# A convolution stem's backward pass: the second input gradient chains its shared products in PSUM, and the order of all operations becomes a written list

## The chip, the cores and the metric

The kernel runs on one core of a Trainium2 chip. The metric is the device time of one execution in microseconds (us), as a median over runs. Five engines work side by side and meet through semaphores: TensorE (PE: matmuls into PSUM, with its weight loads, PEld), VectorE (DVE), ScalarE (ACT), GpSimd (POOL) and SyncE (SP). In this kernel SP issues nearly all DMAs and DMA transposes, POOL the stores of transposed gradient pieces (`dld`). Each engine works through its own instructions in the order in which they were written.

## The reference

A strided one-dimensional convolution with group norm (one group a channel) and GELU, and its vector-Jacobian product:

```python
# x (2, 16000, 256), w (31, 256, 256), grad_out (2, 7985, 256), all bf16
h = sum(einsum('blc,cd->bld', x[:, i:i + 2*L:2, :], w[i]) for i in range(31))   # L = 7985
mu, var = mean and variance of h over l, for each b and d
out = gelu((h - mu) / sqrt(var + 1e-5) * gn_gamma + gn_beta)                   # tanh form
_out, _vjp = jax.vjp(_f, x, w, gn_gamma, gn_beta)
return (out, *_vjp(grad_out))          # out, d/dx, d/dw, d/dgamma, d/dbeta
```

## The kernel before, in words

The program has five stages, which are also the names in its planner: F0 and F1 (forward convolution of batch elements 0 and 1), G0 (the elementwise GELU work and input gradient of element 0), G1 (input gradient of element 1, from the end of element 0's on) and W (the weight gradient). Elementwise work of one stage runs under the matmuls of another.

**The input gradient** (`input_grad`) runs over 2 batch elements, 4 chunks `c`, 2 halves `pr` and 3 branches in the order B, A, C: 24 branches for each element. The convolution is split by fast-convolution identities: a branch has three leaves B, A, C, where leaf B is shared and the results are "B plus A" and "B plus C"; the outputs of branch B are in turn added to those of the branches A and C. `g_sums` makes the differences of input planes on DVE (`first`, `second`, `third`, all through L1282). `slots4` gives each branch two PSUM slots of two banks each, `px` and `pt`; four slots rotate, so a branch uses again what the branch two before it used, with the two slots exchanged.

For a branch of element 0 the steps are: `g_three_b`, four matmuls of 512 columns into the first bank of `px`, and an ACT copy of that bank to the second one (L1356); `g_three_ac`, eight matmuls of difference terms on both banks; `g_seed`, here one ACT copy of `px` into `pt`; then, inside the next branch's steps, `last(A)` and `last(C)`, which add the leaves A and C and evacuate them with `g_evac`: branch B's results into an fp32 tile `GRB` (ACT), the others by a DVE addition with `GRB` into the output tile `HO` (L1428). After branch C the tile goes out in one DMA of 1 MB.

For element 1 (`GOC` holds all its halves) the leaves A and C are split once more: `g_outer` makes a shared product of four matmuls for each of them (with weight sums `W2DO` and `W2DC`, made by `w2_outer`), into the two banks of `pt`, and eight matmuls of difference terms replace sixteen. `g_seed` then joins everything on DVE in fp32: an operation of 2048 elements that adds `GRB` to both products, spread over both banks (in branch B an ACT copy, L1392, instead), and one of 2048 that adds `px` and writes `pt` and `px` (both L1396). As `GRB` is already in the seed, `g_evac` is a plain ACT copy to `HO` (`keep`, L836). A branch has 36 matmuls.

**The order.** The code above only lists operations with their dependencies (`plan.add`). `Plan.order` gave each a due time, from a cost model and two long tables of leads per kind (`lead`, `fine`), and `listing` laid out the five engines by due time in a small model of the chip. `emit` then writes them in that order, so the list fixes the order on each engine. PE runs through helpers with one line per stage: L741 forward, L1329 input gradient, L1564 weight gradient. L683 and L687 are weight differences and sums, L699 the forward's plane sums, L1101 to L1129 the GELU unit, L1211 to L1231 `e_comp`, the elementwise gradient of a half-tile: two loads (`hd`, `dyd`), scalings (on ACT for the last two chunks of element 1, L1218 and L1220), an addition, four copies into the plane tile (L1231). For element 1 all half-tiles share one pair of load buffers, so a load waits until the last of these four copies has read it. L547 is any load or store, L552 a DMA transpose.

## Time and profile before

| what | us |
|---|---|
| runs: lowest, median, highest of 3 | 1164.47, 1166.46, 1167.01 |
| profiled execution: its span, first to last instruction | 1161.2 |
| what lies around the span, against the median of the runs | 5.3 |
| PE busy, DVE busy, ACT busy, POOL busy | 1128.5, 982.8, 554.0, 131.7 |
| matmuls of the input gradients (L1329), first and last start | 417.8, 847.3 |
| `g_seed` on DVE (L1396), first and last start | 655.3, 838.8 |

The profiled execution's own device time is not listed apart from its span; the three runs lie 3.3 to 5.8 us above it. The page gives each engine's busy time, the span in 40 slices, the DMA queues, the chain of work that ended last, and the costliest groups of instructions; the trace behind it answers further views: groups by line and shape (busy us, mean ns of one, idle time before them and what ended it), waits (who waited for whom), the chain of waits in order of time, the timeline (with the idle time before an instruction in brackets) and busy times in windows. Matmuls are pipelined and their ends are modelled.

### The profile page before, as it was taken

To read this page: it belongs to the slowest core of one execution; us is meant where nothing else is said; L and a number is where in the kernel's file an instruction comes from. 1 tells how busy PE (TensorE), PEld (TensorE's weight loads), DVE (VectorE), ACT (ScalarE), POOL (GpSimd) and SP (SyncE) were. 2 spreads that over 40 slices of the span, in tenths; PEclk is the share of its full clock that TensorE was granted. 3 is DMA by queue.
4 is the path that set the end of the run, shared out by engine and by line. 5 is a ranking of instruction groups with operands and counts; after the bars stand their busy time and mean duration, and the time that the engine had idled before them with its cause. 6 is when DMAs were issued, how large, how long until landed. Compare 5 with 4: busy or idle time off the path is not lost.

```text
span 1161.2 us, 18913 instructions
## 1 busy us (share of the span) xinstructions
PE 1128.5 (97%) x7700; PEld 753.2 (65%) x7700; DVE 982.8 (85%) x892; ACT 554.0 (48%) x833; POOL 131.7 (11%) x221
## 2 busy tenths in 40 slices
PE   5999999999999999999899999999999999999998
PEld 3888899877777864444344444444488766656685
DVE  7996787699989988998786868768799998699986
ACT  1254454688786588788563545653422212211200
POOL 0000000000000011333232132241200000000000
PEclk9999999999999999999999999999999999999999
DMA  9476738869796699999996886686999726899673
GB/s 217 63 184 127 179 109 164 208 140 200 182 248 141 221 366 255 261 263 231 256 228 192 179 191 163 159 200 175 212 353 289 256 82 221 287 323 320 219 222 104
DMA packets 345807, 243.57 MB, mean 210 GB/s; under 512 B 233377, under 2 KB 316967, under 8 KB 341543
## 3 DMA queue, kind: packets, MB, share of 16 engines
q1 hardware_dynamic: 338615, 223.47, 73.5%
q0 software_dynamic: 7104, 18.89, 6.1%
q8 instruction: 60, 0.98, 0.4%
q14 instruction: 28, 0.23, 0.1%
HBM read 106.24 MB, written 80.25 MB: 161 GB/s over the span
## 4 chain that ended last, share of the span: by engine, by line
PE 80%; DVE 6%; DMA 6%; ACT 3%; SPq 3%; issue 2%; DVEq 0%; ACTq 0%
PE ps L741 33%; PE ps L1329 24%; PE ps L1564 22%; DMA arena<-dld 2%; SPq L547 2%; DMA out_dram<-arena 1%; DMA arena<-hd 1%; SPq L552 1%; DVE arena L1428 1%; ACT arena L836 1%; DMA arena<-dyd 1%; DVE arena L1116 1%; DVE arena L1282 1%; DVE arena L687 1%; DMA arena<-in_x_dram 1%
## 5 line engine op out<-in xcount | busy, mean ns | idle before, releaser
L1329 PE MATMUL ps<-arena 128*128 128x512 bf16 (+1 forms) x1920 | 414.0, 377 | 9.8 <-DVE arena L1428 3.2
L741 PE MATMUL ps<-arena 128*128 128x256 bf16 (+4 forms) x3460 | 406.8, 281 | 14.7 <-DMA arena<-in_x_dram 6.0
L741 PEld LDWEIGHTS <-arena 128*128 128x128 bf16 x3460 | 338.1, 99 | 83.2 <-DVE arena L683 6.4
L1329 PEld LDWEIGHTS <-arena 128*128 128x128 bf16 x1920 | 188.3, 98 | 233.6 <-issue 16.9
L1564 PE MATMUL ps<-arena 128*128 128x256 bf16 (+1 forms) x2320 | 309.2, 296 | 4.1 <-DMA arena<-dld 2.3
L1564 PEld LDWEIGHTS <-arena 128*128 128x128 bf16 x2320 | 226.8, 98 | 86.8 <-DMA arena<-dld 2.1
L836 ACT ACTIVATE arena<-ps 128x1024 f32<-128x1024 f32 (+1 forms) x111 | 113.1, 1022 | 248.9 <-PE ps L1564 86.1
L699 DVE TENSOR_TENSOR arena<-arena 128x2080 bf16<-128x2080 bf16 (+8 forms) x126 | 157.1, 1266 | 27.1 <-PE ps L741 26.4
L547 POOL DMA_DIRECT2D dld<-arena x144 | 104.6, 728 | 295.1 <-DMA arena<-arena 247.8
L1116 DVE TENSOR_TENSOR arena<-arena 128x2048 bf16<-128x2048 bf16 (+1 forms) x80 | 95.6, 1196 | 11.9 <-ACT arena L1110 5.8
L1282 DVE TENSOR_TENSOR arena<-arena 128x1032 bf16<-128x1032 bf16 (+1 forms) x120 | 84.5, 727 | 12.7 <-PE ps L1329 6.6
L1532 DVE TENSOR_TENSOR arena<-arena 128x4096 bf16<-128x4096 bf16 x38 | 86.1, 2285 | 7.9 <-DMA arena<-in_x_dram 5.5
L1396 DVE TENSOR_TENSOR ps<-ps,arena 128x2048 f32<-128x2048 f32 x24 | 55.1, 2298 | 22.3 <-PE ps L1329 21.4
L856 ACT ACTIVATE arena<-ps 128x512 bf16<-128x512 f32 (+1 forms) x64 | 37.0, 580 | 57.9 <-PE ps L741 53.7
L556 POOL MEMSET arena<- 128x128 bf16 (+11 forms) x40 | 8.6, 246 | 403.6 <-ACT ps L777 149.3
L1666 ACT COPY ps<-ps 128x256 f32<-128x256 f32 x54 | 19.3, 358 | 73.2 <-PE ps L1564 72.1
L1396 DVE TENSOR_TENSOR arena<-ps,arena 128x2048 f32<-128x2048 f32 x16 | 36.6, 2290 | 18.7 <-ACT arena L836 15.3
L1356 ACT COPY ps<-ps 128x512 f32<-128x512 f32 x48 | 27.5, 577 | 44.5 <-PE ps L1329 38.6
L1106 DVE SCALAR_TENSOR_TENSOR arena<-arena 128x2048 bf16<-128x2048 bf16 (+1 forms) x16 | 35.8, 2238 | 12.1 <-ACT arena L1103 12.1
L1428 DVE TENSOR_TENSOR arena<-ps,arena 128x1024 bf16<-128x1024 f32 x32 | 38.8, 1219 | 7.7 <-DMA out_dram<-arena 4.6
L1735 DVE TENSOR_TENSOR arena<-arena 128x4608 bf16<-128x4608 bf16 x16 | 40.5, 2552 | 5.7 <-PE ps L1564 5.6
L777 ACT ACTIVATE ps<-ps 128x256 f32<-128x256 f32 x75 | 27.8, 371 | 36.4 <-PE ps L741 35.1
(83 smaller groups left out, 780.4 us busy)
## 6 DMA issues: line engine op xcount, KB each, us to landing
arena<-in_x_dram SPq DMA_DIRECT2D x40, 1024.0 KB
dld<-arena POOLq DMA_DIRECT2D x144, 128.0 KB, 3.8
arena<-hd SPq DMA_DIRECT2D x32, 512.0 KB
out_dram<-arena SPq DMA_DIRECT2D x14, 1024.0 KB
arena<-dld SPq DMA_DIRECT2D x18, 640.0 KB
arena<-dld SPq DMA_DIRECT2D x18, 576.0 KB
vl<-arena SPq DMA_DIRECT2D x36, 256.0 KB
arena<-vl SPq DMA_DIRECT2D x9, 1024.0 KB
```

What stands on the lines that cost most here:

```text
L547: lambda: e.dma_start(out=out, in_=in_), dma=np_ * ns / 16e3 * 1.03, ns=ns, tp=SH[pk], slack=slack)
L699: lambda: nc.vector.tensor_tensor(out=o, in0=a, in1=b, op=ALU.add))
L741: yield nc.tensor.matmul(ps[:, dh, cs], lhsT=wt, rhs=mv, start=s0, stop=False, skip_group_check=True)
L836: lambda: nc.scalar.activation(out=out, in_=ps, func=ACT.Copy, scale=scale))
L1116: add("DVE", dve(nf), [o], [a, b_], lambda: V.tensor_tensor(out=o, in0=a, in1=b_, op=op))
L1282: lambda: nc.vector.tensor_tensor(out=o, in0=a, in1=b, op=ALU.subtract))
L1329: yield nc.tensor.matmul(ps[:, e, 0:wide], lhsT=lt, rhs=mv, start=s0, stop=False, skip_group_check=True)
L1396: lambda: nc.vector.tensor_tensor(out=o, in0=a, in1=b, op=ALU.add))
L1428: lambda: nc.vector.tensor_tensor(out=ho[:, :, k, :], in0=ps[:], in1=g, op=ALU.add))
L1532: add("DVE", dve(4096), [o], [a, b], lambda: nc.vector.tensor_tensor(out=o, in0=a, in1=b, op=ALU.add))
L1564: yield nc.tensor.matmul(ps[:, s, c0:c1], lhsT=lt, rhs=mv, start=s0, stop=False, skip_group_check=True)
L1735: add("DVE", dve(4608), [o], [u, v], lambda: nc.vector.tensor_tensor(out=o, in0=u, in1=v, op=ALU.subtract))
```

## The change

For element 1, a branch now runs like this. The C product (with `W2DC`) goes into the first bank of `pt`; ACT copies it into the first bank of `px` (`g_copy`). `g_three_b` adds its four matmuls onto that copy (`fresh` is false) and ACT copies the sum to the second bank of `px`. The A product, with weights that are now negated sums, is added onto the C product in `pt`, so that `pt` holds C minus A; ACT copies that to SBUF (`g_delta`, two fp32 tiles `GSD` in turn). After the difference terms, one DVE operation of 1024 elements writes `pt` = `px` minus `GSD`. The branch sums leave the seed: branch B is evacuated into a bf16 tile `GSB`, the others into `HO` by ACT as before, and after leaf C one DVE addition in bf16 of 2048 elements adds `GSB` to the branch's two slices of `HO`. There are two `HO` tiles for element 1; element 0 keeps to one. All of `second` and the joined `third_two` (both leaves' differences in one DVE instruction of 2064 elements) are listed ahead of the first product. Matmuls per branch stay 36. `w2_outer(A)` uses a negating scalar_tensor_tensor instead of an addition. Switches that were empty (`GLAST`) are gone.

The planner's tables and model are gone too. `SEQUENCE` is a written list of all 3252 operations, by their number in the order in which the code adds them (there were 3224), and `order` returns it. It differs from the order before in every stage, forward and weight gradient included.

```diff
+SEQUENCE = """
+6 12 5 7 13 9 4 11 8 17 1 22 16 2 15 14 32 35 31 34 38 40 33 37 36 41 25 42 39 43 44 26 47 46 50 45 49 52 53 27 51 54 55 56 30 48 62 23 67 66 24 61
+29 68 87 28 86 85 18 89 84 20 88 72 21 19 75 59 64 65 58 83 60 73 92 63 57 93 69 91 94 95 179 70 90 177 71 79 236 100 74 97 101 78 102 96 103 10 111
...
+2043 2008 2018 2007 2055 2044 2079 2045 2019 2046 2013 2118 2012 2119 2015 2011 2017 2127 2009 2016 2080 2048 1470 2021 2123 2010 2026 2121 2004 2022
+2120 2049 2023 2050 2028 2024 2025 2060 2051 2207 2061 2052 2020 2030 2053 2054 2027 2031 2206 2131 2032 1477 2029 2036 2126 2033 2062 2122 2076 2211
...
     def order(self):
...
+        seq = [int(i) for i in SEQUENCE.split()]
+        assert sorted(seq) == list(range(len(self.ops)))
+        seen = set()
+        for i in seq:
+            assert self.ops[i]["preds"] <= seen
+            seen.add(i)
+        return seq
...
+    HO = [sb(119232, 2, 4, 512), sb(GREG + 16704, 2, 4, 512)]
+    GSB = sb(115136, 2, 2, 512)
+    GSD = [sb(o, 512, dt=FP32) for o in (111040, 113088)]
...
-    def g_three_b(ps, br, lf, pl, o):
+    def g_three_b(ps, br, lf, pl, o, fresh=True):
...
-        g_mm(ps, jobs, [ps[:, 0]], [wd, pl[1]])
-        add("ACT", act(512), [ps[:, 1]], [ps[:, 0]],
-            lambda: nc.scalar.copy(out=ps[:, 1], in_=ps[:, 0]))
+        g_mm(ps, jobs, [ps[:, 0]], [wd, pl[1]] + ([] if fresh else [ps[:, 0]]))
+        g_copy(ps[:, 1], ps[:, 0])
+
+    def g_copy(o, i):
+        add("ACT", act(512), [o], [i], lambda: nc.scalar.copy(out=o, in_=i))
...
+        jobs = [(0, 512, pl[1][:, dh, o + q2:o + q2 + P], wd[:, dh, 1 - q2, :], lf == C_ and q2 + dh == 0)
                 for q2 in range(2) for dh in range(2)]
-        g_mm(pt, jobs, [pt[:, k]], [wd, pl[1]])
+        g_mm(pt, jobs, [pt[:, 0]], [wd, pl[1]] + ([] if lf == C_ else [pt[:, 0]]))
...
+    def g_delta(pt):
+        gsc[0] += 1
+        g_copy(GSD[gsc[0] % 2], pt[:, 0])
+
+    def g_seed(px, pt, both):
+        if not both:
+            keep(flat2(pt), flat2(px))
+            return
+        t = GSD[gsc[0] % 2]
+        i = bass.AP(tensor=t.tensor, offset=t.offset, ap=[list(t.ap[0]), [0, 2], [1, 512]])
+        add("DVE", dve(1024, 1), [pt[:]], [px[:], t],
+            lambda: nc.vector.tensor_tensor(out=pt[:], in0=px[:], in1=i, op=ALU.subtract))
...
         if both:
...
             keep(ho[:, :, k, :], ps[:])
+            if lf == C_:
+                v, g = ho[:, :, r2:r2 + 3:2, :], GSB.rearrange("p l e f -> p e l f")
+                add("DVE", dve(2048), [v], [v, GSB], lambda: nc.vector.tensor_tensor(out=v, in0=v, in1=g, op=ALU.add))
...
+                        if both:
+                            if pr == 0:
+                                second(br, C_)
+                                second(br, A)
+                                third_two(br)
+                            g_outer(pt, br, planes(br, C_), o, C_)
+                            g_copy(px[:, 0], pt[:, 0])
+                        g_three_b(px, br, B_, planes(br, B_), o, not both)
...
+                        if both:
+                            g_outer(pt, br, planes(br, A), o, A)
+                            g_delta(pt)
+                        g_three_ac(px, br, B_, GU[br], o)
```

In the list's first two lines, 61 to 85 are the first weight differences and plane sums of the forward pass (83 is the weight difference that PE's matmul group 92 reads, 63 the one that 90 and 91 read). In the two lines further down stands the first branch of element 1: 2021 is its C product and 2022 the copy, 2023 the B product and 2024 the copy, 2028 the A product and 2029 the copy, 2030 and 2031 the difference terms, 2036 the subtraction; 2025, 2026, 2032 and 2033 are the leaves of the branch before (eight matmuls each, as that branch is of element 0) and 2034 the evacuation of its leaf C; 2068, 2075 and 2076 are leaf groups of this branch (four matmuls each); 2051 to 2054 are the four copies of an `e_comp`, 2206 and 2207 the loads of the half-tile after it, 2211 one of its scalings; 2064, in the line after these, is the next branch's C product.

470 lines of the change are left out of this document (40 added, 430 removed), and 98 rows, old and new, of the table SEQUENCE.

## The prediction

> **What bounds the kernel now.** I read the page's head first, then the waits of TensorE (PE) over the whole span, the busy times in windows of 50 us over the second input gradient, the groups by line and shape, and last the timeline and the chain of waits at the places where PE stood still.
>
> ```profile
> span 1161.2 us, 18913 instructions
> PE 1128.5 (97%) x7700; PEld 753.2 (65%) x7700; DVE 982.8 (85%) x892; ACT 554.0 (48%) x833; POOL 131.7 (11%) x221
> ```
>
> PE is busy for 97% of the span, and the change leaves its matmuls alone. So VectorE (DVE) time is worth something only where PE waits for DVE. These are PE's waits (us in total, times, longest):
>
> ```profile
> PE ps L741 <- DMA arena<-in_x_dram: 6.0, 2, 4.6
> PE ps L741 <- DVE arena L683: 5.6, 1, 5.6
> PE ps L1329 <- DVE arena L1428: 3.2, 1, 3.2
> PE ps L1329 <- ACT ps L836: 3.1, 2, 1.8
> PE ps L1329 <- ACT arena L836: 2.4, 3, 1.9
> PE ps L1564 <- DMA arena<-dld: 2.3, 2, 1.6
> PE ps L741 <- DVE arena L699: 1.9, 1, 1.9
> ...
> PE ps L1329 <- DVE ps L1396: 0.3, 1, 0.3
> ```
>
> Three rows (6.0, 5.6, 1.9) belong to the first 23 us. Of what is left, 3.2 + 3.1 + 2.4 + 2.3 + 0.3 = 11.3 us stand here, and the six short rows left out (0.7, 0.7, 0.6, 0.6, 0.5, 0.4) add 3.5: 14.8 us in all. For the DVE work that the change cuts, L1396, PE waited 0.3 us. The windows of the second gradient say the same (PE, PEld, DVE, ACT busy us of 50, with counts):
>
> ```profile
> 650.00:700.00 50.00, 47.76 (x223) 21.55 (x222) 36.30 (x31) 29.09 (x34) 16.34 (x25) 1.00 0.82 180
> 700.00:750.00 50.00, 49.75 (x233) 22.60 (x232) 41.22 (x37) 28.50 (x34) 13.36 (x22) 1.00 0.68 175
> 800.00:850.00 50.00, 47.24 (x237) 22.84 (x235) 37.78 (x26) 19.79 (x24) 11.58 (x16) 1.00 0.94 232
> ```
>
> In 700 to 750, 233 matmuls fill 49.75 us: 0.2135 us each at a granted clock of 1.00. I count PE time below in matmuls of 0.2135 us. PE's idle time is in 650 to 700 (2.24 us) and 800 to 850 (2.76 us). The Trainium skill (Perfetto Trace Analysis, Identifying the Most-Contended Engine) holds matmul busy time to be a bad measure of headroom and names LDWEIGHTS busy share and MFU instead. By the first (22.60 of 50) more than half of this window would be free; the even 0.2135 us of the row speak for 0.25 us free, and the row decides.
>
> **The change part by part.** First the engines (mean ns of one behind the busy time):
>
> ```profile
> L1396 DVE TENSOR_TENSOR ps<-ps,arena 128x2048 f32<-128x2048 f32 x24 | 55.1, 2298 | 22.3 <-PE ps L1329 21.4
> L1396 DVE TENSOR_TENSOR arena<-ps,arena 128x2048 f32<-128x2048 f32 x16 | 36.6, 2290 | 18.7 <-ACT arena L836 15.3 <-PE ps L1329 3.2
> L1392 ACT COPY arena<-ps 128x2048 f32<-128x2048 f32 x8 | 14.9, 1867 | 4.8 <-PE ps L1329 4.1 <-DVE ps L1396 0.8
> L821 DVE TENSOR_TENSOR ps<-ps,arena 128x1024 f32<-128x1024 f32 x28 | 34.1, 1226 | 6.9 <-PE ps L1564 5.9 <-ACT arena L836 1.0
> L1634 DVE TENSOR_TENSOR arena<-arena 128x2048 bf16<-128x2048 bf16 x32 | 37.9, 1219 | 0.2
> L1356 ACT COPY ps<-ps 128x512 f32<-128x512 f32 x48 | 27.5, 577 | 44.5 <-PE ps L1329 38.6 <-DVE arena L1213 5.8
> L811 ACT ACTIVATE arena<-ps 128x512 f32<-128x512 f32 x56 | 29.8, 600 | 29.4 <-PE ps L741 17.2 <-DVE ps L821 10.2 <-DVE arena L821 1.9
> L836 ACT ACTIVATE arena<-ps 128x1024 bf16<-128x1024 f32 x32 | 32.7, 1024 | 48.6 <-PE ps L1329 48.4
> L1231 ACT COPY arena<-arena 128x768 bf16<-128x768 bf16 x32 | 25.6, 829 | 11.9 <-DVE arena L1222 7.4 <-POOL arena L556 4.5
> L1231 ACT COPY arena<-arena 128x256 bf16<-128x256 bf16 x32 | 11.7, 402 | 0.0
> L1220 ACT ACTIVATE arena<-arena,stats 128x1024 bf16<-128x1024 bf16 x8 | 8.9, 1140 | 6.9 <-DMA arena<-dyd 6.9
> ```
>
> DVE loses all of L1396, 55.1 + 36.6 = 91.7 us. It gains one subtraction of 1024 in each of the 24 branches (priced as L821: 24 x 1.226 = 29.4) and 16 additions of 2048 in bf16 (as L1634: 16 x 1.219 = 19.5). That is -42.8 us of DVE. Joining two difference planes into one instruction (12 fewer) saves little and I leave it out; the three negated weight sums become another operation on 2048 elements, at L1396's full 2.29 against 1.22 that is 1.07 us more each, and in the trace nobody waits for the sums that they replace. ScalarE (ACT) loses L1392, 14.9 us, and gains two copies of 512 a branch: 24 x 0.577 + 24 x 0.600 = 28.2, so +13.3 us. Of the stretch from 650 to 840 us that is 7 points of ACT, which stood between 40 and 58%. PE keeps its 36 matmuls a branch. The direct gain of the DVE saving is the 0.3 us that PE waited for L1396. No DMA is added or removed; the second output tile takes away a wait that no row of this stage shows, and counts nothing.
>
> Now the new chain. In a branch PE makes the C product, ACT copies it, PE adds the B product upon it, ACT copies that, PE adds the eight matmuls of the difference terms; the negated A product is chained on the C product and copied out; DVE subtracts, and the leaves follow. What an uncovered copy costs is in the trace:
>
> ```profile
> 834.95 0.57 ACT L1356 COPY ps<-ps 128x512 f32<-128x512 f32 x1 [3.35 <-PE ps L1329]
> 835.57 5.13 PE L1329 MATMUL ps<-arena 128*128 128x512 bf16 x24 [0.71 <-ACT ps L1356]
> ```
>
> A copy of 0.57 us with nothing to cover it keeps PE idle for 0.71 us. I read the list branch by branch for the matmuls of other groups that it puts between. Between the C product and the B product there are 4 in two branches and 8 to 20 in the other 22 (median 8, 1.71 us); between the B product and the term that reads the second copy at least 8; between the last difference term and the first leaf at least 8 (median 14, 3.0 us) against one subtraction of 1.23 us. Four matmuls are 0.85 us, 0.14 above the exposed copy, so none of these is exposed while ACT is free. The banks turn round more tightly than before: the C product, now first of its branch, writes the bank whose leaf came last two branches earlier, with 8 matmuls (1.71 us) between in most branches, against an evacuation of 1.02 us (L836) and the same 0.14. Margin 0.55 us. With ACT busy about 60% of this stretch, some will find another operation ahead: I take +0.5 us over 24 branches (between 0 and 24 x (0.83 - 0.55) = 6.7, where every branch finds one copy of L1231 ahead).
>
> Then the order, which is new in every stage, so each wait of the table has to be asked. Four transfers on the chain of waits (start, us, what) stand behind four of them:
>
> ```profile
> 547.38 8.65 DMA out_dram<-arena
> ...
> 679.96 4.55 DMA arena<-hd
> ...
> 689.04 7.55 DMA arena<-dyd
> ...
> 831.17 11.11 DMA arena<-dld
> ```
>
> The longest of the L836 waits, 1.9 us: ACT stood at a scaling whose load took 7.55 us, with an evacuation behind it that PE needed. In the list this half-tile has 60 matmuls (12.8 us) of PE work from the earliest issue of the load to the product that needs the evacuation: two copies, load, scaling, evacuation make about 0.7 + 1.7 + 7.55 + 1.14 + 1.02 = 12.1, so this wait goes. But the half-tile before it gets worse. There ACT's entries run 2024, 2051 to 2054, 2029, 2211, 2034: 2054 frees the buffer that load 2206 fills, 2211 scales it, 2034 evacuates the bank of C product 2064. From the end of 2023 ACT needs 0.7 + 2 x 0.83 + 2 x 0.4 = 3.2 us, the load 4.55 (the row of hd, the same size) to 7.55, then 1.14 and 1.02: 9.9 to 12.9 us. PE has 44 matmuls between 2023 and 2064, 9.4 us. I take +1.9 out of 0.5 to 3.5: -1.9 + 1.9 = 0.
>
> The 3.2 us of L1428 is an output store of 8.65 us that had to land before the one output tile was written again. The first gradient keeps one tile; the list gives this store 62 matmuls of work instead of 58: -0.9 (4 x 0.2135). Other stores get less (50 and 54 for 70 and 74), so the bounds are -3.2 and +3.2. The 1.6 us before the first matmul of the weight gradient is a load of 11.11 us; the list puts 60 matmuls (12.8 us) between its issue and its use instead of 39 (8.4): -1.6; the load used next has 28 instead of 32 and is what could be late then. The two ACT waits of 3.1 us at the end of the GELU work have no row that says what the new order makes of them: -1.5, bounds -3.1 and +3.1.
>
> ```profile
> 12.66 2.39 DVE L699 TENSOR_TENSOR arena<-arena 128x2080 bf16<-128x2080 bf16 x2
> 14.96 1.22 DVE L683 TENSOR_TENSOR arena<-arena 128x2048 bf16<-128x2048 bf16 x1
> 16.09 1.23 DVE L699 TENSOR_TENSOR arena<-arena 128x2064 bf16<-128x2064 bf16 x1
> 17.24 13.70 DVE L683 TENSOR_TENSOR arena<-arena 128x2048 bf16<-128x2048 bf16 x12
> 23.06 7.13 PE L741 MATMUL ps<-arena 128*128 128x256 bf16 x48 [5.63 <-DVE arena L683]
> ```
>
> At the start PE waits until the fifth of the twelve: nine long sums stand before it. In the list eight do (68, 85, 84, 72, 75, 64, 65, 83), -1.1 us, but the next weights (63) then come one sum later than they did behind 83, and PE would wait some 0.5 there: -0.6.
>
> The sum: -0.3 (L1396) + 0.5 (copies and banks) + 0 (loads ahead of ACT) - 0.9 (store) - 1.6 (first weight-gradient load) - 1.5 (GELU end) - 0.6 (start) = -4.4 us. The profiled span 1161.2 becomes 1156.8. The runs shown have a median of 1166.46, 5.3 above the span; with that kept, 1162.1.
>
> **The rivals.** *No change.* The DVE saving is off PE's path, and the waits that the list removes come back elsewhere. For it: DVE's 91.7 us cost PE 0.3. Against it: the first load of the weight gradient and the start have plain room. Time: 1166.5, within 2.3 either way.
>
> *The list does much more.* Its order is free in every stage, and all 14.8 us of waits behind the start could go: 1151.7. For it: every wait outside the start is a single event of 1 to 3 us. Against: the half-tile above.
>
> *Slower: ACT's queue decides.* PE now needs three copies of ACT in each branch where it needed one, and ACT works in order. Before, a scaling that waited 6.9 us for its load (the L1220 row) cost PE 1.9. If both half-tiles of this chunk stop ACT for 6.9 us, with 1.7 us of cover before PE stands, PE pays 5.2 twice, and where the copies collide 24 x 0.28 = 6.7 at most, half of it taken: 10.4 - 1.9 = 8.5 for the loads and 3.4 for the copies in place of the 0 and 0.5 of my sum: -4.9 + 8.5 + 3.4 = +7.0, 1173.5; with the loads alone -4.4 + 8.5 = +4.1, 1170.6. It decides once the two half-tiles together cost PE over 6.3 us (1.9 as now, and the 4.4 of the sum). The Trainium skill (PSUM — Partial Sum Buffer, PSUM bank collisions raise a hardware error) wants PSUM guarded by bank: while ACT copies a bank, PE may not write any of it. By this both products behind a copy are serial, which would be 24 x 2 x 0.71 = 34 us if nothing stood between; the 0.71 us row shows such a wait, and the list's 4 to 20 matmuls are why I don't take it.
>
> *The weight-gradient and forward stages lose in the new order*, for reasons that no row shows: about +4 us, 1170.
>
> **How the numbers follow.** A measurement of this kernel can tell about 0.2% (2.3 us) from no change. My forecast, 3 to 8 us faster, gets 0.45; much more 0.16; no change 0.21; ACT's queue 0.11; the other stages 0.07. Faster by over 0.2%: 0.45 + 0.16 = 0.61; within: 0.21; slower: 0.18. The likeliest one's own range is 1158 to 1164; the range for 8 in 10 goes from just above the full removal, 1153, to the price of the other stages and of the loads alone, 1170.
>
> **What would show it.** In the profile of the changed kernel: DVE 41 to 44 us less busy, ACT about 13 more, PE the same; L1396's successor at 1.23 us x24; PE's wait for copies and evacuations in 650 to 840 us under 3 us; no wait for the first load of the weight gradient; PE's start wait under 5.6 us. Wrong would be PE waits for ACT of 5 us and more behind a scaling that waits for a load (then ACT's queue decides), or new waits in the forward pass or the weight gradient.

## The result and the profile after

The changed kernel takes 1147.09 us (median of 4 runs, 1147.02 to 1148.26); the kernel before, run beside it, 1165.47 us (4 runs, 1164.16 to 1167.01). The ratio is 0.9833, 95% interval 0.981 to 0.9857: 18.4 us or 1.7% faster. The direction was forecast, the size was not: 1162.1 with a range from 1153.

The head of the page of the changed kernel:

```profile
span 1145.0 us, 18889 instructions
PE 1121.4 (98%) x7645; PEld 753.0 (66%) x7700; DVE 943.7 (82%) x880; ACT 561.7 (49%) x873; POOL 129.2 (11%) x221
```

The profiled run took 1147.09 us, so 2.1 us lie around its span. (55 of the 7700 matmul records are missing, which takes some us off PE's busy time; all weight loads are there.) DVE is 39.1 us less busy, ACT 7.7 more. PE's waits, all of them (us in total, times, longest):

```profile
PE ps L504 <- DVE arena L446: 6.6, 2, 4.2
PE ps L504 <- DMA arena<-in_x_dram: 5.5, 2, 4.6
PE ps L1311 <- DVE arena L1477: 2.6, 1, 2.6
PE ps L1099 <- DVE arena L1180: 0.5, 1, 0.5
PE ps L1099 <- ACT ps L599: 0.4, 1, 0.4
PE ps L1311 <- DVE arena L1381: 0.3, 1, 0.3
```

L504 (forward), L1099 (input gradient) and L1311 (weight gradient) are the lines that were L741, L1329 and L1564; L446 was L683, L599 was L836, L1180 was L1428. The first two rows are the start of the program. Behind it, 14.8 us in fifteen waits have become 3.8 us in four, and one of these, 2.6 us behind L1477, is new. The groups of the new branch (busy us, mean ns, idle before):

```profile
L1162 DVE TENSOR_TENSOR ps<-ps,arena 128x1024 f32<-128x1024 f32 x24 | 29.5, 1231 | 59.0 <-PE ps L1099 36.3
L1128 ACT COPY ps<-ps 128x512 f32<-128x512 f32 x72 | 41.5, 577 | 28.4 <-PE ps L1099 25.5
```

Both are as priced, 1.231 us for the subtraction and 0.577 for a copy; the 72 copies are 48 from PSUM for element 1 and 24 for element 0. Neither line has a row in PE's waits. The timeline of PE says the same of the whole second gradient in one line: one piece without a pause, from 639.7 to 828.9 us.

```profile
639.69 189.25 PE L1099 MATMUL ps<-arena 128*128 128x512 bf16 x865
```

The windows by stage, of the kernel before and then of the changed one (start:end, length, then PE, PEld, DVE, ACT and POOL busy, granted clock, DMA share, GB/s):

```profile
421.00:654.00 233.00, 226.65 (x1061) 104.13 (x1060) 193.89 (x236) 161.26 (x195) 64.90 (x99) 0.99 0.95 242
654.00:844.00 190.00, 184.89 (x862) 84.15 (x861) 142.67 (x110) 99.06 (x112) 53.80 (x87) 1.00 0.79 187
```

```profile
418.00:643.00 225.00, 223.00 (x1038) 103.49 (x1058) 195.22 (x232) 161.65 (x198) 61.04 (x98) 1.00 0.95 252
643.00:828.00 185.00, 184.04 (x848) 84.63 (x865) 101.89 (x104) 110.68 (x151) 56.66 (x90) 1.00 0.75 193
```

In the second gradient PE stood for 5.1 us of 190 and now for 1.0 of 185. In the first, 6.4 of 233 have become 2.0 of 225, though its code is the same.

For all kernels below I cut the span at the start of weight load 3460 (the number of the forward's), 4516, 5380 and 7700, the last. At the cuts up to 16 loads of the next stage stand among those of the one before, so a part is good to about 1 us.

| kernel | forward | first gradient | second gradient | weight gradient | span |
|---|---|---|---|---|---|
| before | 421.5 | 232.3 | 190.5 | 312.5 | 1161.2 |
| changed | 418.2 | 225.2 | 185.0 | 311.6 | 1145.0 |
| changed, again (e15) | 418.9 | 225.1 | 185.0 | 311.5 | 1145.6 |
| e1 new arithmetic, planner | 422.9 | 238.0 | 191.9 | 337.1 | 1194.3 |
| e2 old arithmetic, list | 418.0 | 226.4 | 257.5 | 323.4 | 1230.2 |
| e2b the same, first seed earlier | 418.7 | 226.3 | 255.6 | 323.8 | 1229.4 |
| e6 old arithmetic, list but for element 1 | 420.0 | 248.1 | 187.4 | 313.5 | 1173.9 |
| e6b old arithmetic, list then planner | 417.9 | 228.9 | 189.1 | 310.8 | 1151.1 |
| e3 changed, planner in the forward | 424.3 | 227.1 | 184.8 | 311.5 | 1152.8 |
| e4 changed, planner in element 0's gradient | 423.6 | 234.8 | 184.8 | 312.8 | 1161.1 |
| e7 new arithmetic, planner then list | 422.2 | 241.8 | 184.8 | 312.6 | 1166.4 |
| e8 subtraction twice | 418.2 | 225.1 | 206.4 | 312.9 | 1167.5 |
| e9 copies twice | 417.8 | 225.3 | 203.8 | 313.0 | 1164.9 |
| e11 plane differences twice | 418.5 | 226.4 | 204.9 | 312.6 | 1167.5 |
| e10 one output tile | 419.8 | 225.1 | 192.5 | 320.8 | 1163.2 |
| e12 tiles swapped | 417.6 | 225.2 | 184.8 | 316.1 | 1148.8 |
| e13 swapped, store earlier | 418.9 | 225.1 | 184.8 | 310.9 | 1144.7 |
| e14 store earlier | 418.7 | 225.3 | 185.0 | 312.6 | 1146.6 |

So the 16.2 us of the span are 3.3 in the forward, 7.1 in the first gradient, 5.5 in the second and 0.9 in the weight gradient, less 0.7 behind the last load. Nearly two thirds come from the forward and the first gradient, whose arithmetic the change leaves alone. The table compares one execution of each kernel. In 69 other runs of the kernel before the time is 1.7 to 1.9 us above the span, so its 1161.2 stand for about 1163.0 us, less than any of the four runs beside the changed kernel; of the 18.4 us between the medians the table explains 16.2.

### The profile page after: what moved, and what is told of

The parts are those of the page before. It is cut to its first block, busy times and chain, and to the rows that moved or that the text cites. A ratio compares the mean times of both kernels' runs of the same rounds, so it can differ in the third digit from the quotient of the medians.

```text
span 1145.0 us, 18889 instructions
## 1 busy us (share of the span) xinstructions
PE 1121.4 (98%) x7645; PEld 753.0 (66%) x7700; DVE 943.7 (82%) x880; ACT 561.7 (49%) x873; POOL 129.2 (11%) x221
## 4 chain that ended last, share of the span: by engine, by line
PE 89%; DVE 7%; ACT 1%; issue 1%; DMA 1%; SPq 0%; DVEq 0%; ACTq 0%
PE ps L504 34%; PE ps L1099 33%; PE ps L1311 22%; DVE arena L1279 1%; DVE arena L1397 1%; DVE ps L1421 1%; DVE arena L1381 1%; DMA out_dram<-arena 1%; DVE arena L1045 1%; DMA arena<-in_x_dram 1%; DVE arena L446 0%; DVE arena L1482 0%; DVE arena L462 0%; ACT arena L994 0%; DVE arena L879 0%
## 5 line engine op out<-in xcount | busy, mean ns | idle before, releaser
L504 PE MATMUL ps<-arena 128*128 128x256 bf16 (+4 forms) x3460 | 406.0, 281 | 12.1 <-DVE arena L446 6.6
L1099 PE MATMUL ps<-arena 128*128 128x512 bf16 x1880 | 408.2, 377 | 3.0 <-DVE arena L1180 0.5
L504 PEld LDWEIGHTS <-arena 128*128 128x128 bf16 x3460 | 338.2, 98 | 79.8 <-DVE arena L446 7.0
L1099 PEld LDWEIGHTS <-arena 128*128 128x128 bf16 x1920 | 188.0, 98 | 222.5 <-issue 2.3
L1311 PE MATMUL ps<-arena 128*128 128x256 bf16 (+1 forms) x2305 | 307.8, 296 | 3.7 <-DVE arena L1477 2.6
L1311 PEld LDWEIGHTS <-arena 128*128 128x128 bf16 x2320 | 226.8, 98 | 84.8 <-issue 3.0
L599 ACT ACTIVATE arena<-ps 128x1024 f32<-128x1024 f32 (+1 forms) x111 | 112.6, 1023 | 234.4 <-PE ps L1311 82.8
L462 DVE TENSOR_TENSOR arena<-arena 128x2064 bf16<-128x2064 bf16 (+8 forms) x126 | 155.7, 1266 | 17.1 <-PE ps L504 16.0
L1279 DVE TENSOR_TENSOR arena<-arena 128x4096 bf16<-128x4096 bf16 x38 | 86.4, 2289 | 12.4 <-DMA arena<-in_x_dram 7.8
L1045 DVE TENSOR_TENSOR arena<-arena 128x1032 bf16<-128x1032 bf16 (+1 forms) x108 | 82.2, 791 | 9.7 <-PE ps L1099 9.3
L1162 DVE TENSOR_TENSOR ps<-ps,arena 128x1024 f32<-128x1024 f32 x24 | 29.5, 1231 | 59.0 <-PE ps L1099 36.3
L1128 ACT COPY ps<-ps 128x512 f32<-128x512 f32 x72 | 41.5, 577 | 28.4 <-PE ps L1099 25.5
L574 ACT ACTIVATE arena<-ps 128x512 f32<-128x512 f32 x56 | 30.6, 601 | 44.2 <-PE ps L504 30.5
L869 DVE SCALAR_TENSOR_TENSOR arena<-arena 128x2048 bf16<-128x2048 bf16 (+1 forms) x16 | 35.8, 2240 | 16.7 <-ACT arena L864 10.7
L1180 DVE TENSOR_TENSOR arena<-ps,arena 128x1024 bf16<-128x1024 f32 x32 | 38.9, 1220 | 8.5 <-PE ps L1099 6.4
L1397 DVE TENSOR_TENSOR arena<-arena 128x2048 bf16<-128x2048 bf16 x36 | 43.4, 1222 | 0.1
```

The costliest lines, as they stand in the source:

```text
L462: lambda: nc.vector.tensor_tensor(out=o, in0=a, in1=b, op=ALU.add))
L504: yield nc.tensor.matmul(ps[:, dh, cs], lhsT=wt, rhs=mv, start=s0, stop=False, skip_group_check=True)
L599: lambda: nc.scalar.activation(out=out, in_=ps, func=ACT.Copy, scale=scale))
L1045: lambda: nc.vector.tensor_tensor(out=o, in0=a, in1=b, op=ALU.subtract))
L1099: yield nc.tensor.matmul(ps[:, e, 0:wide], lhsT=lt, rhs=mv, start=s0, stop=False, skip_group_check=True)
L1128: add("ACT", act(512), [o], [i], lambda: nc.scalar.copy(out=o, in_=i))
```

## The experiments

My theory after the result: the order is what gains, by taking away the single waits in every stage, and in the second gradient the lighter chain is what lets such an order exist. The rival: the lighter chain gains by itself. "The planner" below is the order of before, "the list" that of the change; "arithmetic" is the code of the second gradient.

### Order or arithmetic: e1, e2, e2b

The new arithmetic under the old planner and its tables (e1); the old arithmetic in the list's order, with both seed operations where the list has the subtraction (e2), or with the first of them where the list has the copy of `pt` (e2b). The edits, against the changed kernel and against the kernel before:

```diff
-SEQUENCE = """
...
-        seq = [int(i) for i in SEQUENCE.split()]
...
+        self.look = 13
+        self.pads = (3122.5, 3149.5, 2842.0)
+        self.lead = {
...
+        self.listing(due, succ)
+        return sorted(range(n), key=lambda i: (self.start[i], i))
```

```diff
+SEQUENCE = """
...
-        self.listing(due, succ)
-        return sorted(range(n), key=lambda i: (self.start[i], i))
...
+        seq = [int(i) for i in SEQUENCE.split()]
...
```

> The new arithmetic of the second input gradient, ordered by the planner of before with its tables (the list left out). Theory A (the written order makes the gain, in every stage): about the time of before, 1158 to 1168 us, with waits of the matmul engine for the output store, the GELU work's ACT and the first weight-gradient load back. Theory B (the lighter arithmetic makes it, by freeing VectorE): 1147 to 1152 us.

> The arithmetic of before, in the order of the new list: every operation that both kernels have at its place in the list, the seed's two operations of a branch at the place of the subtraction, and moved later where a dependency asks for it. Theory A (order): 1147 to 1154 us. Theory B (arithmetic): 1160 to 1167 us, the seeds of 2.3 us holding up the tightly packed second gradient.

> The arithmetic of before in the list's order, with the first of the two seed subtractions at the place that the copy of the shared second difference has in the list, and the second at the place of the one subtraction. Theory A (the list holds exactly eight matmuls under one subtraction of 1.2 us; two chained ones of 1.1 and 1.2 us with the old copies don't fit, wherever the first of them stands): the forward and the first gradient end as in the changed kernel (643 to 645 us), the second input gradient takes over 200 us, and the time is over 1163 us. Theory B (the long second gradient of the first such run came from the place of the first subtraction alone): the second input gradient takes 185 to 191 us and the time is 1147 to 1155 us; then the order would be the whole gain.

e1: 1198.25 us (ratio 1.031, 1.0266 to 1.0354). e2: 1232.36 (1.0596, 1.0559 to 1.0634). e2b: 1231.31 (1.0553, 1.0526 to 1.0581). Each half of the change alone is slower than no change; e1 and e2 lie above the ranges of both theories, e2b is as its first theory had it. In e1 the second gradient takes 191.9 us: with the lighter seed and the old planner it gains nothing. Its other losses lie elsewhere, most of them in the weight gradient (337.1). That the tables of leads were made for other operations is the likely reason; no run shows it. Three of PE's waits in e1:

```profile
PE ps L1549 <- DVE ps L1659: 7.9, 5, 2.5
PE ps L1549 <- DMA arena<-dld: 6.7, 1, 6.7
PE ps L1337 <- ACT ps L1366: 5.5, 7, 1.2
```

The last row is the exposed copies (L1366 is the copy there), the cost that I had bounded with 6.7.

e2 and e2b have the forward and the first gradient of the changed kernel (418.0 and 418.7, 226.4 and 226.3) with the old arithmetic: there the order is the whole gain, to about 1 us. In the second gradient the same list takes 70 us more than with the new arithmetic. PE's waits in e2b, and its window:

```profile
PE ps L1301 <- DVE ps L1368: 42.3, 17, 7.0
PE ps L1536 <- ACT arena L808: 9.6, 1, 9.6
PE ps L1301 <- DVE arena L1254: 9.5, 6, 3.3
```

```profile
640.00:900.00 260.00, 207.32 (x881) 89.20 (x880) 155.48 (x126) 99.21 (x112) 56.38 (x92) 0.91 0.54 141
```

L1368 is the old seed. In the changed kernel the list has exactly eight matmuls (1.71 us) between the last difference term and the first leaf in 18 of 24 branches and 12 to 20 in the others; the order of before had 12 to 36. One subtraction of 1.23 us fits under eight, two operations of 2.3 don't. The clock of 0.91 tells that the waits cost a second time: 9% of 260 us is 23 us at full speed. That the place of the first seed operation isn't the cause is shown by e2b against e2. What a list made for the old arithmetic would give was not tried.

### Stage by stage: e6, e6b, e7, e3, e4

e6b has the old arithmetic, the list up to the first product of element 1 and the planner's order behind it; e7 the new arithmetic and the reverse, planner first and list behind. e6 was an earlier form of e6b that chose by stage name and so mixed the two orders. e3 and e4 are the changed kernel with the operations of the forward (e3) or of element 0's gradient (e4) at the planner's places. Only `SEQUENCE` differs from the changed kernel, in e7 and e3 from its first entries on (or, in e6 and e6b, as in e2):

```diff
-6 12 5 7 13 9 4 11 8 17 1 22 16 2 15 14 32 35 31 34 38 40 33 37 36 41 25 42 39 43 44 26 47 46 50 45 49 52 53 27 51 54 55 56 30 48 62 23 67 66 24 61
...
+5 10 12 0 22 13 6 7 11 8 9 14 1 4 15 2 16 3 17 31 32 34 35 37 33 38 40 36 41 23 39 42 43 44 24 46 47 49 45 50 52 48 53 25 51 54 55 56 61 27 66 28 67
...
```

> The arithmetic of before; the list for the forward stages, the GELU work with the first gradient and the weight gradient; the planner's own order of before for the second gradient. If order and arithmetic only pay together in the second gradient: about 10 us of the gain (forward 3.3, first gradient 7.2) without the new arithmetic, 1152 to 1156 us, with the second gradient taking its 190 us as before. If the arithmetic is needed everywhere: 1160 us or more.

> The arithmetic of before throughout; the operations up to the first product of element 1's input gradient (forward products, GELU, first input gradient) in the list's order, everything behind that in the planner's order, so that the two orders meet at one place. Theory A (what the list gains before the second input gradient doesn't depend on the new arithmetic): the second input gradient's first product comes at about 643 us as in the changed kernel instead of 654, the second input gradient takes the 190 to 193 us of before, and the time is 1153 to 1157 us. Theory B (that gain comes only together with the lighter second input gradient, or is paid back behind the meeting place): 1160 us or more, with the second input gradient or the weight gradient longer than before by what was gained.

> The new arithmetic; the planner's order up to the first product of element 1's input gradient, the list behind it. Theory A (the order gains apart in each stage): the second input gradient takes 185 to 186 us as in the changed kernel instead of 190.5, the weight gradient as in the changed kernel, the forward and the first gradient as before (654 us or a little more for the seam): 1156 to 1160 us. Theory B (the gain of the second input gradient comes from how far ahead the list has run by then): its 185 us are lost and the time is 1163 us or more.

> The changed kernel with the operations of the forward stages (F0, F1) put back to the places that the planner of before gave them, counted in matmul work done before them; all others as in the list. Theory A (order): the forward part loses its 3.3 us, 1150 to 1151 us. Theory B: no change from 1147 us.

> The changed kernel with the operations of stage G0 (GELU work of element 1 and first input gradient) put back to the places that the planner of before gave them; all others as in the list. Theory A (order): the 7.2 us that this stage gained are lost, about 1154 us, with the waits for the output store and for ACT back and a stretch at half the matmul clock behind the longest. Theory B: no change from 1147 us.

e6b: 1155.58 us (0.9923, 0.9893 to 0.9952). About 9 of the 18 us need no new arithmetic at all. At the place where the orders meet PE waits once, 3.6 us (first row); its second gradient takes 189.1 us, and the waits in it are the other three rows:

```profile
PE ps L1301 <- DVE arena L1400: 4.1, 2, 3.6
PE ps L1536 <- DMA arena<-dld: 2.6, 1, 2.6
PE ps L1301 <- ACT arena L808: 0.7, 3, 0.2
PE ps L1301 <- ACT ps L1328: 0.7, 1, 0.7
```

The 1.9 us behind L836 that stood in this stage before isn't among them, with the same arithmetic and the planner's order. So of the 4.1 us between 189.1 and the changed kernel's 185.0, 2.6 are the wait for the first load of the weight gradient (the changed kernel's wait of the same size, behind L1477, falls behind the cut), and only 1.4 are waits of the gradient itself. That is what list and new arithmetic together save inside the stage beside e6b; beside the one profile of before it looks like 5.5.

e6 at 1176.75 (1.0114, 1.008 to 1.0149) lies in the range of the theory that the arithmetic is needed, but says little for it: PE waited four times, 14.4 us together, for output tiles whose stores the mixed order held back, and its second gradient, with the old arithmetic, takes 187.4 us.

e7: 1168.35 (1.0037, 1.0013 to 1.0062). The second gradient takes the list's 184.8 us, so it doesn't matter how the program came there; but the first gradient takes 241.8, 9.5 more than before, where the planner's order for new operations waits 6.0 us for an output tile (L1180) and 3.1 for sums (L1045). The total fell in the range of the theory that the stage refutes. e3: 1156.37 (0.9942, 0.9918 to 0.9967), above the 1150 to 1151 expected, 6 us lost in the forward, 2 in the first gradient, none behind. e4: 1162.70 (0.9983, 0.9962 to 1.0004), above the 1154 expected, 9.6 lost in the first gradient and 5.4 in the forward, under which element 0's elementwise work runs. In all three the second gradient is 184.8. Part of each loss is the seam between two orders; the second gradient's time doesn't hang on what stands ahead of it.

### How tight the list is: e8, e9, e11

The changed kernel, with one kind of work of element 1 written twice (the same values again, nothing left out): the subtraction (e8), the three ACT copies of each branch (e9), the plane differences, which are off the chain (e11).

```diff
+        def go():
+            for _ in range(2):
+                yield nc.vector.tensor_tensor(out=pt[:], in0=px[:], in1=i, op=ALU.subtract)
+        add("DVE", dve(1024, 1), [pt[:]], [px[:], t], go)
```

```diff
+        g_copy(ps[:, 1], ps[:, 0], 1 if fresh else 2)
...
+    def g_copy(o, i, n=2):
+        def go():
+            for _ in range(n):
+                yield nc.scalar.copy(out=o, in_=i)
+        add("ACT", act(512), [o], [i], go)
```

```diff
+            def go():
+                for _ in range(1 if t < 4 else 2):
+                    yield nc.vector.tensor_tensor(out=o, in0=a, in1=b, op=ALU.subtract)
+            add("DVE", dve(o.free_size()), [o], [a, b], go)
```

> The changed kernel with the subtraction of each of the 24 branches written twice, the same values both times: 1.23 us more on the chain from the difference terms to the first leaf, and 29.5 us more of VectorE. If the short chain is what lets the list run tight: waits where the list has only 8 matmuls of cover (1.71 us) against two subtractions (2.46), 9 of 24 branches by 0.8 us, plus half-clock stretches: 1152 to 1160 us. If there is slack: 1147 to 1149 us.

> The changed kernel with the three ACT copies of each branch of element 1 written twice: 0.58 us more between the C product and the B product, the same before the difference terms and the subtraction, 42 us more of ACT. By the prediction's count of cover (at least 1.71 us against 1.3 in 22 of 24 branches, 0.85 in two): 1148 to 1150 us. If ACT's queue decides, as the slower rival had it: 1155 us or more.

> The changed kernel with every plane difference of element 1 written twice, the same values both times: about 41 us more of VectorE in the second gradient, as much as the change freed, on work that is made ahead and not on the chain of seed and leaf. If freed VectorE time is what pays: 1152 us or more. If only the chain's length counts: 1147 to 1149 us.

e8: 1169.67 (1.0044, 1.0025 to 1.0063), second gradient +21.4 us. e9: 1167.23 (1.002, 0.9999 to 1.0042), +18.8. e11: 1170.13 (1.0063, 1.0041 to 1.0086), +19.9. e8 lies above both of its ranges, e9 and e11 in those of ACT's queue and of the freed VectorE time. Each of the three alone gives back all that the change brought. The rows of PE's waits for the doubled work, of e8, e9 and e11:

```profile
PE ps L1099 <- DVE ps L1164: 17.8, 21, 1.1
```

```profile
PE ps L1099 <- ACT ps L1130: 10.7, 15, 1.7
...
PE ps L1099 <- DVE ps L1165: 3.4, 8, 0.7
```

```profile
PE ps L1101 <- DVE ps L1164: 12.3, 6, 4.7
```

In e8, 21 of 24 branches wait, together 17.8 us, so 0.85 each of the 1.23 added: the cover left over is 0.3 to 0.4 us a branch, as 1.71 of matmuls over 1.23 of subtraction and the hops around it suggests. (21 is the number of branches with 8 or 12 matmuls of cover; the expectation had counted 9 with 8.) e11 is the surprise. Its added differences are made ahead of their use (PE waits once, 0.3 us, for such a difference), and in the changed kernel DVE was busy for only 106 us of the 190 from 640 to 830. DVE's busy time grew by 50 us, some 44 of them in this stage, and PE waits up to 4.7 us: in DVE's fixed order the subtraction stands behind them. At the longest wait DVE works through twelve differences, 9.31 us, and then the subtraction that PE needs.

### The second output tile and the new wait: e10, e12, e13, e14, e15

e10 uses one output tile for element 1, e12 swaps the turns of the two.

```diff
-        ho = HO[pr if both else 0]
+        ho = HO[0]
```

```diff
-        ho = HO[pr if both else 0]
+        ho = HO[1 - pr if both else 0]
```

> The changed kernel with one output tile for element 1's stores instead of two, the list mended only where the second use of the tile must come after the first store. Theory A (the second tile is what spares TensorE the waits on a store of about 8 us): waits at each of the half columns come back, 2 to 8 us, 1149 to 1155 us. Theory B (the list leaves enough work between an addition and the next use of its tile): within 1 us of the changed kernel, 1146.5 to 1148 us.

> The changed kernel with its two output tiles of element 1 in swapped turns, so that the last store before the weight gradient leaves from the tile that the first rows of the weight gradient don't overlap; the list is the same. Theory (the 2.6 us wait at the start of the weight gradient is the last output store that must land before the difference of its left leaves writes over that tile): the wait goes, the weight gradient starts its products without a pause, 1144.0 to 1145.0 us, ratio to the changed kernel 0.997 to 0.998. Rival (the wait goes to the next thing, an input that lands late or the store of the tile before): 1146.5 to 1147.5 us.

e10: 1164.76 (0.9992, 0.9977 to 1.0006), above both of its ranges. Without the second tile the change is worth nothing. PE's waits in e10:

```profile
PE ps L1311 <- ACT arena L599: 9.6, 1, 9.6
...
PE ps L1099 <- ACT arena L599: 4.8, 2, 4.5
```

L599 evacuates into the tile, and stands until the store has left. (In the list as written, that is, with the few entries moved that one tile asks for; a list made for one tile was not tried.)

e12: 1151.52 (0.9887, 0.9868 to 0.9906), so slower than the changed kernel by 4 us and against both sides of the expectation. The chain of waits of the changed kernel, and of e12, at the start of the weight gradient:

```profile
832.60 6.68 DMA out_dram<-arena
839.29 0.02 issue
839.31 2.63 DVE arena L1477 x2
```

```profile
832.24 8.99 DMA out_dram<-arena
841.23 0.02 issue
841.25 2.64 DVE arena L1477 x2
```

L1477 writes the difference of the left leaves over the second output tile, so it waits for the store from that tile. I had taken the swap to give it an older store. But the timeline of SP in the changed kernel shows the last two stores leaving together, at 832.6:

```profile
832.60 0.75 SPq L311 DMA_DIRECT2D out_dram<-arena  x2
```

The store before the last could leave 18 us earlier (at 814.5, as e13 below shows), but the list puts it among the last entries, just behind the last store. The swap only made L1477 wait for the larger of the two (1 MB instead of 832 KB). So I moved that one entry, 2616, forward, ahead of the last store and four loads (the expectations say two), with the tiles swapped (e13) and not swapped (e14), and ran the changed kernel again beside them (e15):

```diff
-2617 2605 2649 2613 2607 2640 2612 2641 2666 2614 2665 2615 2652 2658 2696 2653 2659 2707 2667 2654 2704 2660 2669 2655 2708 2661 2670 2671 2656 2672
...
+2617 2605 2649 2613 2607 2640 2612 2641 2666 2614 2665 2615 2652 2658 2696 2653 2659 2707 2667 2654 2704 2616 2660 2669 2655 2708 2661 2670 2671 2656
...
```

> The changed kernel with its two output tiles in swapped turns and with one entry of the list moved: the last output store but one, which could leave some 20 us earlier, goes ahead of two loads instead of behind them. Theory (what the difference of the left leaves waits for is the store that leaves from the tile that it overwrites, and this store is late because it stands late in SP's order): the 2.6 us wait goes without another in its place, 1143.5 to 1145.0 us. Rival (an input whose load now stands behind the store comes late): a wait on a load of the weight gradient of 1 us or more, 1146 to 1149 us.

> The changed kernel with its tiles in their own turns and only the last output store but one moved ahead of two loads. Theory (the difference waits for the last store, which lands sooner if it doesn't share the DMA engines with the store before it): the 2.6 us wait becomes 0 to 1.5 us, 1144.5 to 1146.5 us. Rival (the landing time of the last store is its own, not that of the company): the wait stays within 0.5 us of 2.6, 1147 us.

> The changed kernel itself once more, beside these on the same chip: 1146.5 to 1148.5 us by both theories, the wait of 2 to 3 us at the start of the weight gradient again, without or with a stretch of half clock behind it (then 1149 to 1151 us).

e13: 1146.27 us (1146.07 to 1146.79; ratio to before 0.9829, 0.9804 to 0.9854). e14: 1148.76 (1147.21 to 1151.40). e15: 1147.69 (1147.32 to 1149.22). e15 is as expected. In e13 the store leaves at 814.5, the wait for it is gone, and 1.9 us of PE's wait stay:

```profile
L311 SPq DMA_DIRECT2D out_dram<-arena x2: 350/364/377, 814.5 to 833.0; - x2
```

The timeline of DVE in e13 shows why: it works without a pause from the last output addition (L1176) through both pairs of L1477, the second of which PE waits for.

```profile
830.47 2.48 DVE L1176 TENSOR_TENSOR arena<-arena 128x2048 bf16<-128x2048 bf16 x2 [0.78 <-ACT arena L599]
...
835.21 2.62 DVE L1477 TENSOR_TENSOR arena<-arena 128x2304 bf16<-128x2304 bf16 x2
837.94 1.23 DVE L1397 TENSOR_TENSOR arena<-arena 128x2048 bf16<-128x2048 bf16 x1
839.08 2.62 DVE L1477 TENSOR_TENSOR arena<-arena 128x2304 bf16<-128x2304 bf16 x2
```

Behind the transfer stood DVE itself, busy in e13 for 49.39 of the 50 us from 830. All four runs of e13 lie below all five of the changed kernel beside it, 1.4 us by the medians: a version slightly better than both, short of the 2.6 us expected. In e14 the wait fell only from 2.6 to 2.2 us, as its rival had it (within 0.5 us of 2.6), and the clock took that back (below).

## Why the prediction was wrong, point by point

The error is 15.0 us, in two parts. **The time around the span.** I kept 5.3 us, the median's distance from the profiled span, but these belong to different executions. In the 69 runs of before for which time and span are both known, 1.7 to 1.9 us lie around the span, and 2.1 in the profiled run of the changed kernel: 3.2 us of the error. **The sum.** It said -4.4; the span fell by 16.2, which makes 11.8. PE's waits fell by 12.4 us (28.3 to 15.9), the 1.7 us that a stretch at half clock behind one of them had cost went too, and some 2 us stand in no row. The step that failed is the pricing of PE's waits in the new order: where no row spoke for a wait's going, the sum let it stay in part (store, GELU end) or come back (+1.9 ahead of ACT), and 4.7 us of short waits had no term at all. Nearly all went.

- *L1396, -0.3, and copies and banks, +0.5:* no row of either is left in PE's waits. The sizes of the operations were right to 1% (1.231 for 1.226, 0.577 for 0.577). "The direct gain of the DVE saving is the 0.3 us that PE waited for L1396" holds as far as the runs go: in the old order the saving gains nothing (e1: 191.9 after 190.5). One count of the list was wrong: between the last difference term and the first leaf stand 8 matmuls in the median, not 14; the subtraction fits under them all the same. What the prediction doesn't have is that the list is packed so closely that it needs the saving: work given back on the chain costs half to three quarters of itself (e9: 41 us of copies, 18.8; e8: 29.5 us, 21.4), and 50 us given back off the chain cost 19.9 (e11).
- *The waits without a term:* the sum named 10.1 of the 14.8 us (0.3, 1.9, 3.2, 3.1, 1.6). The other 4.7 (the six short rows, 0.7 of a second load, 0.5 of two short waits for L836) it left as they were, without a reason. Of these 0.8 are left, at other places.
- *The second gradient as a whole:* its terms made -1.4 (-0.3, +0.5, 0, and -1.6 for the load at its end); the stage fell by 5.5. The waits that stood in it (2.4 behind L836, 1.6, 0.7, 0.3) are all gone.
- *Loads ahead of ACT, -1.9 + 1.9:* the wait went, its successor didn't come. ACT did stand before the scaling, but for 2.2 us, since the load took about 4 us and not up to 7.55:

```profile
647.69 1.15 ACT L983 ACTIVATE arena<-arena,stats 128x1024 bf16<-128x1024 bf16 x1 [2.21 <-DMA arena<-dyd]
```

- *The output store of the first gradient, -0.9:* all 3.2 us went. I counted matmuls between store and next use, 62 for 58, and didn't look at what stood ahead of the store on SP. The timeline of SP, before and changed:

```profile
539.57 7.70 SPq L552 DMA_TRANSPOSE arena<-in_grad_out_dram  x1
547.38 0.52 SPq L547 DMA_DIRECT2D out_dram<-arena  x1
```

```profile
538.55 3.85 SPq L316 DMA_TRANSPOSE arena<-arena  x3
542.50 0.53 SPq L311 DMA_DIRECT2D out_dram<-arena  x1
```

In both kernels the last addition to the tile starts within 0.2 us of 540.4 and takes 1.2. Before, the store then stood 5.7 us behind one transpose that held SP for 7.70; now it leaves 0.9 us after the addition. That is worth more than twenty matmuls, and not four. Behind this wait the clock had also fallen, which I left out of the price: the window of before from 550 to 600 has 0.97, that is 1.5 us (the record of the granted clock has 3.41 us at half clock, 1.7 us).

```profile
557.40 32.54 PE L1329 MATMUL ps<-arena 128*128 128x512 bf16 x144 [3.15 <-DVE arena L1428]
```

```profile
550.00:600.00 50.00, 45.03 (x204) 20.23 (x203) 37.76 (x40) 30.60 (x33) 14.58 (x22) 0.97 1.02 236
```

- *GELU end, -1.5 of 3.1:* 0.4 left, so -2.7. Half had no reason but the want of a row.
- *First weight-gradient load, -1.6:* it went, as counted. But behind it came the 2.6 us of L1477, which the prediction had not seen: the second output tile, "counts nothing" in it, overlaps what the weight gradient writes first. The one thing that I had named as late next, the load after, wasn't.
- *Start, -0.6:* PE's waits there fell from 13.5 to 12.1, -1.4.
- *Engines:* DVE -39.1 for -41 to -44 (the rows of the changed operations alone sum to about -41; the negated sums cost 2.28 us each, as said); ACT +7.7 for +13 (the rows of the changed operations sum to about +13, but neighbours overlap more in the records). PE alike.
- *The rivals:* "the list does much more" is what happened, at 1151.7 and a chance of 0.16; with the 2.1 around the span it would have said 1148.5. I held against it that waits come back elsewhere, and gave 0.45 to half of them doing so. In fact 13.6 of the 14.8 us went, and 2.6 came new. "ACT's queue decides" rested on two half-tiles and on copies that collide; e9 shows that its mechanism is real (10.7 us of waits for copies), once each copy takes another 0.57 us. By the bank rule (the Trainium skill, PSUM — Partial Sum Buffer, PSUM bank collisions raise a hardware error) a product has to wait for the copy that reads its bank. In the changed kernel each such wait is covered: no row of PE's waits names L1128.

That the order alone gains in the forward and the first gradient is shown (e2, e2b, e6b). That this list can't be used with the old arithmetic in the second gradient is shown too (e2, e2b), and that the new arithmetic gains nothing in the planner's order (e1). How much the new arithmetic is worth there stays open: the planner's order with the old arithmetic has only 1.4 us of waits of its own in e6b, and a list fitted to the old arithmetic was not tried. Open is also how much of e3's, e4's, e6b's and e7's losses is seam.

## What to carry to other kernels

Where one engine is busy for 97% and its waits are single events, price a new order by what stands ahead of each releaser on its own queue (SP too), not by the distance in matmuls alone, and allow that nearly all waits go. Time saved on an engine off the path is worth what an order can make of it: nothing in the old order here, a few us at most in one fitted to it (4.1 beside e6b, 2.6 of them a wait for a load), and that fit leaves 0.3 to 0.4 us of room a branch, so every later edit of the chain must make its order anew. When a wait is removed, ask what its engine had queued behind it: the store's 2.6 us held only 0.7 that weren't DVE's own work.

## What the runs showed of the hardware

**Whether the clock falls behind a wait depends on where the wait lies in a grid of 3.413 us.** Windows of 830 to 880 us, PEclk, in the changed kernel, e14 and e12, where PE waited at 839 us for 2.57, 2.17 and 5.26 us:

```profile
830.00:880.00 50.00, 47.43 (x436) 42.32 (x434) 49.24 (x37) 12.29 (x21) 0.00 (x0) 1.00 0.94 265
```

```profile
830.00:880.00 50.00, 47.83 (x424) 42.08 (x422) 47.61 (x36) 12.97 (x21) 0.00 (x0) 0.97 0.85 252
```

```profile
830.00:880.00 50.00, 44.73 (x388) 38.99 (x386) 44.92 (x35) 11.50 (x20) 0.00 (x0) 0.93 0.81 243
```

By the traces' record of the granted clock the shortest of the three waits brought a stretch of 3.41 us at half clock, the middle one none, the longest 6.83 us. So e14, with less waiting than the changed kernel, had a weight gradient 1 us longer, and e12 one 4.6 us longer than e15 for 2.7 us more of waiting.

In the 18 traces the stretches at half clock begin a whole number of 3.413 us apart (in e2b at 22.23 and 691.24 us, 196.0 times), and all but the last ones, which run past the end of the program, last that long or a multiple of it. So the idle time can be counted in these windows. From 12 us on, the clock fell behind every window at full clock in which PE was idle for more than 2.03 us, and behind none in which it was idle for less than 1.97. (PE's idle time rests on modelled ends.) The 2.17 us of e14 lie in one window; of the changed kernel's 2.57 us 1.79 lie in one and the rest in the next. The Trainium skill (TensorE: Matmul & The Clock Gate, Part 1) has a window of about 3.4 us that runs freely, which these traces show as well, and has the clock fall after such a window of idling; here 2 us of idling in a window were enough.

**A DMA transpose held SP's queue for 7.70 us** (the row at 539.57 us of before, above), with every store and load behind it.
